# Sixteen of 24 attention chunks: q and k transposed by DMA instead of on TensorE

## The chip, the cores and the metric

One core of a Trainium2 chip. The metric is device time in microseconds (us); the kernels are compared in alternating rounds on one chip. A ratio is the mean time of one kernel's fast runs over that of the other's of the same rounds, so it is not quite the ratio of the medians quoted beside it. All profiled runs told of here are in the fast state. In the profile lines PE is TensorE, PEld its weight loads, DVE VectorE, ACT ScalarE, POOL GpSimd and SP SyncE, which here issues DMAs; PSUM is the memory that this kernel's matmuls and transposes on TensorE write to.

## The reference, cut to what matters

Chunked linear attention with decay feeds a two-layer MLP with a piecewise activation:

```python
# B, H, S, D = 4, 8, 768, 64; reference works in blocks of 64, the kernel in chunks of 128 rows
intra = (q_b @ k_b.T * decay_mask) @ v_b          # per batch and head
inter = (q_b * lam_pow) @ kv_state
out   = intra + inter
kv_state = lam_block * kv_state + (k_b * rev_pow).T @ v_b
...
x = out.transpose(0, 2, 1, 3).reshape(3072, 512)
h = x @ w_in                                      # 512 -> 2048
g = where(h >= 1, h, where(h <= -1, 0, (h + 1)**2 / 4))
y = g @ w_out                                     # 2048 -> 512
```

## The kernel before

It has 24 chunks of 128 rows, and 6 MLP stages of 512 rows that take four chunks each. A list scheduler written in Python orders every engine's work before the program is built: each operation has an engine, an estimated duration in ns (plus `extra` until its result is there), the operations that it needs, and a due time. Engines then run their lists in that order. The estimates set the order and nothing else; a wrong one shows later as an engine standing at an instruction that isn't ready, with ready ones behind it (in the changed kernel ScalarE stood for 3.59 us at a v cast, while an eviction behind it had its matmuls done for 2.4 us of that).

```python
def cast(c, x, eng):          # GpSimd from chunk 4 on: q or k times its decay table, f32 -> bf16
    ...
def cast_v(c):                # ScalarE: v to bf16
    nc.scalar.copy(out=v_out(vi[c % NV]), in_=qkv_ld[c, 2].rearrange("p (a b) d -> p a b d", b=2))
def f_t(c):                   # PE: 8 transposes of 128x128 into PSUM
    for i, x in ((1, ks), (0, qs)):
        for hp in range(HP):
            nc.tensor.transpose(out=ptt[c][:, i, hp, :], in_=pair(x[c], hp), identity=ident)
def f_kb(c, hi):              # VectorE: transposed k into a zero-padded tile, twice a chunk
    nc.vector.tensor_copy(kbd[c % NKB][HD[hi], :, hi, :], ptt[c][HD[hi], 1])
def f_qT(c, e):               # VectorE (ScalarE for the first chunks): transposed q to SBUF
    ...
# the plan: loads book 1.19 us of the DMA queue and land 1.4 us after; 6 buffers each for q, k, v
add(("ld", i, x), "DMA", 1190, ..., [("cast", i - LD, x), ...], extra=1400, due=pos_)
add(("cast", c, 2), "ACT", 640, lambda c=c: cast_v(c), [("ld", c, 2), ("o", c - NV), ("u", c - NV), ("cast", c - 1, 2)])
add(("r", n1), "ACT", 690, ...)   # ScalarE: evict one block of the first MLP layer from PSUM
```

All loads of q, k and v and all stores are issued from SP, in one in-order queue (in the changed kernel SP stood for 1.31 us at a transpose whose cast was not done, with the next load behind it); the weights come through GpSimd's queue. ScalarE also evicts every block of both MLP layers, so what stands in front of an eviction on ScalarE can stop PE: the program has two PSUM tiles for the first layer, and in the changed kernel PE waited 2.4 us in all for their evictions `r`.

Of the kernel before, what the change touches and what calls it, by code (L numbers as in the profile page):

```python
# [9 lines left out]
BF16 = mybir.dt.bfloat16  # L10
# [13 lines left out]
def kernel(  # L24
# [16 lines left out]
    nc = tc.nc  # L41
# [3 lines left out]
    HP = H // 2  # L45
# [8 lines left out]
    CPS = MS // C  # L54

    LD = 6
    RW, NR = 2, 3
    DBG = False

    const = ctx.enter_context(tc.tile_pool(name="const", bufs=1))  # L60
    big = ctx.enter_context(tc.tile_pool(name="big", bufs=1))
    ld = ctx.enter_context(tc.tile_pool(name="ld", bufs=LD))
    qkp = ctx.enter_context(tc.tile_pool(name="qkp", bufs=3))
    qtp = ctx.enter_context(tc.tile_pool(name="qtp", bufs=3))
    scp = ctx.enter_context(tc.tile_pool(name="scp", bufs=3))
    xp = ctx.enter_context(tc.tile_pool(name="xp", bufs=3))
    gp = ctx.enter_context(tc.tile_pool(name="gp", bufs=2))
# [31 lines left out]
        out=causal, in_=causal, compare_op=AX.is_ge, fill=0.0,  # L99
# [3 lines left out]
    NKB, NUB, NV = 3, 3, 4  # L103
    kbd = [const.tile([128, HP, 2, 128], BF16, name=f"kbd{i}") for i in range(NKB)]
# [47 lines left out]
    LAT, FILL = 70, 170  # L152
# [6 lines left out]
    def add(key, eng, ns, fn, needs=(), due=None, extra=0):  # L159
        OPS[key] = Op(key, eng, ns, fn, needs, due, extra)  # L160
        ops.append(OPS[key])

    def run_plan(free):
# [36 lines left out]
        for t, _, x in sorted(out_seq, key=lambda p: p[:2]):  # L200
            if DBG:
                print(f"{t / 1e3:9.3f} {x.due / 1e3:9.3f} {x.eng:5s} {x.ns:6.0f} {x.key}")
            x.fn()

    def mm(*cols):
        return sum(c / 2.4 + 3 for c in cols)


    qs, ks, qT, sc_sb, xT, ptt, pst, pot = {}, {}, {}, {}, {}, {}, {}, {}
    pu = [None]  # L210
    HD = [slice(0, 64), slice(64, 128)]

    def pair(t, hp):
        return t[:, 2 * hp:2 * hp + 2, :].rearrange("p a d -> p (a d)")

    def cast(c, x, eng):
        tab, d, nm = ((tab_q, qs, "qs"), (tab_k, ks, "ks"))[x]
        t = qkp.tile([128, H, D], BF16, name=nm, tag=nm)
        eng.tensor_tensor(t, qkv_ld[c, x], _bc(tab[:, c % NCB, :], 2, D), op=AX.mult)  # L219
        d[c] = t  # L220

    def cast_v(c):
        nc.scalar.copy(out=v_out(vi[c % NV]), in_=qkv_ld[c, 2].rearrange("p (a b) d -> p a b d", b=2))  # L223

    def f_t(c):
        ptt[c] = pp_t.tile([128, 2, HP, 128], BF16, name="pt", tag="pt")
        for i, x in ((1, ks), (0, qs)):
            for hp in range(HP):
                nc.tensor.transpose(out=ptt[c][:, i, hp, :], in_=pair(x[c], hp), identity=ident)  # L229

    def f_kb(c, hi):
        nc.vector.tensor_copy(kbd[c % NKB][HD[hi], :, hi, :], ptt[c][HD[hi], 1])  # L232

    def f_qT(c, e):
        qT[c] = qtp.tile([128, HP, 128], BF16, name="qT", tag="qT")
        (nc.scalar.copy if e == "ACT" else nc.vector.tensor_copy)(qT[c], ptt[c][:, 0])  # L236

    def f_u(c):
        if c % NCB == 0:
            pu[0] = pp_u.tile([128, HP, 128], F32, name="pu", tag="pu")  # L240
        for hp in range(HP):
            nc.tensor.matmul(pu[0][:, hp, :], lhsT=pair(ks[c], hp), rhs=v_pair(vi[c % NV], hp),  # L242
                             start=(c % NCB == 0 and hp == 0), stop=True, skip_group_check=True)

    def f_ub(c, hi):
        nc.scalar.copy(out=ubd[c % NUB][HD[hi], :, HD[hi]], in_=pu[0][HD[hi], :, HD[hi]])

    def f_s(c, g):
        pst[c, g] = pp_s.tile([128, 4, 128], F32, name="ps", tag="ps")
        for j in range(2):  # L250
            for hi in range(2):
                nc.tensor.matmul(pst[c, g][:, 2 * j + hi, :], lhsT=kbd[c % NKB][:, 2 * g + j, hi, :],  # L252
                                 rhs=qT[c][:, 2 * g + j, :], start=True, stop=True)

    def f_m(c, g):
        if g == 0:
            sc_sb[c] = scp.tile([128, 2 * HP, 128], BF16, name="sc", tag="sc")
        nc.vector.tensor_tensor(sc_sb[c][:, 4 * g:4 * g + 4, :], pst[c, g], _bc(causal, 1, 4), op=AX.mult)  # L258

    def f_o(c):  # L260
        cb = c % NCB
        po = pot[c] = pp_o.tile([128, HP, 128], F32, name="po", tag="po")
        for hp in range(HP):
            if cb > 0:
                nc.tensor.matmul(po[:, hp], lhsT=ubd[(c - 1) % NUB][:, hp, :], rhs=qT[c][:, hp, :],  # L265
                                 start=True, stop=False)
            for hi in range(2):
                nc.tensor.matmul(po[:, hp], lhsT=vi[c % NV][:, hp, hi].rearrange("p a d -> p (a d)"),  # L268
                                 rhs=sc_sb[c][:, 2 * hp + hi, :], start=(cb == 0 and hi == 0), stop=(hi == 1))

    def f_x(c):
        sx, off = c // CPS, (c % CPS) * C
        if sx not in xT:
            xT[sx] = xp.tile([128, KO, MS], BF16, name="xT", tag="xT")
        nc.scalar.copy(out=xT[sx][:, :, off:off + C], in_=pot[c])  # L275
# [77 lines left out]
    def o_due(c):  # L353
        s, i = c // CPS, c % CPS
        if s == 0:
            return T0 - LEAD - (CPS - 1 - i) * 3550
        if s in QS:
            return l_due[1, s, 0, i] - LEAD
        return first[s] - LEAD - (CPS - 1 - i) * (first[s] - first[s - 1]) / CPS
# [12 lines left out]
    for kind, i in order:  # L372
        if kind == "w":
            for j in range(WS):
                add(("wi", i, j), "POOL", 900, lambda i=i, j=j: (load_w_in, load_w_out)[i](j),
                    [("cast", CPS - 2 + min(j, 1), 0), ("cast", CPS - 2 + min(j, 1), 1), ("wi", i, j - 1)] if i == 0 else [("cast", CPS, 1), ("cast", CPS, 0) if j else None, ("wi", i, j - 1)],
                    due=j + 4 * i)
# [9 lines left out]
    for c in range(NCH):  # L387
        od, cb = o_due(c), c % NCB
        lastu = c - 1 if cb else c - 2
        for x in (1, 0):  # L390
            e = "DVE" if c < CPS and x == (0 if c == CPS - 1 else 1) else "POOL"
            add(("cast", c, x), e, 690 if e == "DVE" else 1060,
                lambda c=c, x=x, eng=(nc.vector if e == "DVE" else nc.gpsimd): cast(c, x, eng),
                [("ld", c, x), ("t", c - 3), ("u", c - 3), ("cast", c - 1, x)])
        add(("cast", c, 2), "ACT", 640, lambda c=c: cast_v(c),
            [("ld", c, 2), ("o", c - NV), ("u", c - NV), ("cast", c - 1, 2)])
        add(("t", c), "PE", mm(*[128] * 8), lambda c=c: f_t(c),
            [("cast", c, 0), ("cast", c, 1), ("kb", c - 1, 0), ("kb", c - 1, 1), ("qT", c - 1)], due=od - 6000, extra=FILL)
        for hi in range(2):
            add(("kb", c, hi), "DVE", 365, lambda c=c, hi=hi: f_kb(c, hi), [("t", c), ("s", c - NKB, 1)])  # L400
        e = "ACT" if c < CPS else "DVE"
        add(("qT", c), e, 600 if c < CPS else 365, lambda c=c, e=e: f_qT(c, e), [("t", c), ("o", c - 3), ("qT", c - 1)])
        if cb < NCB - 1:
            add(("u", c), "PE", mm(*[128] * 4), lambda c=c: f_u(c),
                [("cast", c, 1), ("cast", c, 2), ("ub", lastu, 0), ("ub", lastu, 1), ("u", lastu)], due=od - 4000, extra=FILL)
            for hi in range(2):
                add(("ub", c, hi), "ACT", 372, lambda c=c, hi=hi: f_ub(c, hi), [("u", c), ("o", c - NUB + 1)])
        for h in range(2):
            add(("s", c, h), "PE", mm(*[128] * 4), lambda c=c, h=h: f_s(c, h),
                [("kb", c, 0), ("kb", c, 1), ("qT", c), ("m", c, 0) if h else ("m", c - 1, 1)],  # L410
                due=od - 3000 + 1000 * h, extra=FILL)
            add(("m", c, h), "DVE", 690, lambda c=c, h=h: f_m(c, h), [("s", c, h), ("o", c - 3), ("m", c, 0) if h else None])
        add(("o", c), "PE", mm(*[128] * (12 if cb else 8)), lambda c=c: f_o(c),
            [("m", c, 1), ("cast", c, 2), ("ub", c - 1, 0) if cb else None, ("ub", c - 1, 1) if cb else None,
             ("x", c - 1), ("o", c - 1)], due=od, extra=FILL)
        add(("x", c), "ACT", 600, lambda c=c: f_x(c), [("o", c), ("x", c - 1), ("l1", (c // CPS - 2) * FO - 1)])
# [65 lines left out]
```

## Time and profile before

| | before |
|---|---|
| time, median of 4 runs | 238.21 us |
| span of the profiled run | 234.8 us |
| PE slots in the program (worked out as in the prediction, 0.0563 us for 128 columns, 0.2163 us for 512) | 208.8 us |
| span less slots: PE waiting, start and end included | 26.0 us |
| ScalarE waiting for v loads, 60 to 165 us | 2.7 us |

"Span less slots" is the figure to follow through this document. The change takes 7.2 us of slots away; whatever else happens to the time is a change in PE's waiting. The profiled run of this kernel was the shortest of its four (236.26 us), so differences from its 26.0 us can be up to about 2 us too large. The page's own lines are in the prediction. One view that the prediction did not show is ScalarE's waits between 60 and 165 us (who waited for whom: us in total, times, longest):

```profile
ACT vi_127 L223 <- DMA x2f<-in_v_dram: 1.1, 2, 0.7
ACT vi_129 L223 <- DMA x2f<-in_v_dram: 1.0, 1, 1.0
ACT vi_126 L223 <- DMA x2f<-in_v_dram: 0.6, 1, 0.6
```

`x2f` is the loaded v and `vi` its cast: before the change ScalarE hardly ever reaches a v cast ahead of its load.

### The profile page before, as it was taken

To read this page: it belongs to the slowest core of one execution; us is meant where nothing else is said; L and a number is where in the kernel's file an instruction comes from. 1 tells how busy PE (TensorE), PEld (TensorE's weight loads), DVE (VectorE), ACT (ScalarE), POOL (GpSimd) and SP (SyncE) were. 2 spreads that over 40 slices of the span, in tenths; PEclk is the share of its full clock that TensorE was granted. 3 is DMA by queue.
4 is the path that set the end of the run, shared out by engine and by line. 5 is a ranking of instruction groups with operands and counts; after the bars stand their busy time and mean duration, and the time that the engine had idled before them with its cause. 6 is when DMAs were issued, how large, how long until landed. Compare 5 with 4: busy or idle time off the path is not lost.

```text
span 234.8 us, 4665 instructions
## 1 busy us (share of the span) xinstructions
PE 213.8 (91%) x1876; PEld 137.1 (58%) x1904; DVE 160.3 (68%) x274; ACT 123.4 (53%) x216; POOL 59.4 (25%) x64
## 2 busy tenths in 40 slices
PE   0487997999997999999999999999999999999993
PEld 0476633575896997777765455555555454444441
DVE  7587399957499999885776876876766835545300
ACT  3456566243577766666566366566455354544110
POOL 6562071061366548303303403302000000000000
PEclk9999999999999999999999999999999999999999
DMA  6999969986999999899993011011011011110212
GB/s 139 220 212 200 192 112 185 196 162 186 247 201 218 227 221 206 191 243 228 230 255 81 19 45 37 12 45 47 0 45 47 0 45 47 45 43 2 92 51 83
DMA packets 82725, 29.67 MB, mean 126 GB/s; under 512 B 75536, under 2 KB 79632, under 8 KB 82704
## 3 DMA queue, kind: packets, MB, share of 16 engines
q1 hardware_dynamic: 78336, 25.17, 48.2%
q0 software_dynamic: 4224, 4.19, 11.1%
q8 instruction: 15, 0.25, 0.4%
q14 instruction: 6, 0.05, 0.1%
q10 hardware_dynamic: 144, 0.00, 0.0%
HBM read 27.27 MB, written 6.29 MB: 143 GB/s over the span
## 4 chain that ended last, share of the span: by engine, by line
PE 75%; DVE 16%; ACT 3%; DMA 2%; issue 2%; SPq 0%; ACTq 0%
PE py L323 33%; PE ph L295 26%; PE ps L252 5%; DVE gT L315 4%; PE pt L229 4%; PE po L268 4%; DMA x2f<-in_v_dram 2%; DVE sc L258 2%; PE pu L242 2%; PE po L265 2%; ACT r L303 1%; DVE kbd_121 L232 1%; PE ph L288 1%; DVE kbd_120 L232 1%; DVE qT L236 1%
## 5 line engine op out<-in xcount | busy, mean ns | idle before, releaser
L303 ACT ACTIVATE r<-ph,one 128x512 bf16<-128x512 f32 x94 | 64.1, 687 | 57.6 <-PE ph L295 40.9
L295 PE MATMUL ph<-xT,w_in_sb 128*128 128x128 bf16 (+1 forms) x744 | 93.1, 269 | 1.0 <-ACT r L303 0.4
L323 PE MATMUL py<-w_out_sb,gT 128*128 128x512 bf16 x364 | 91.5, 379 | 0.9
L295 PEld LDWEIGHTS <-w_in_sb 128*128 128x128 bf16 x752 | 53.0, 98 | 28.0 <-issue 1.4
L323 PEld LDWEIGHTS <-gT 128*128 128x128 bf16 x384 | 35.4, 98 | 33.3 <-DVE gT L315 0.2
L219 POOL TENSOR_TENSOR ks<-x1f,tab_k 128x512 bf16<-128x512 f32 x21 | 24.0, 1141 | 93.0 <-DMA x1f<-in_k_dram 38.9
L258 DVE TENSOR_TENSOR sc<-ps,causal 128x512 bf16<-128x512 f32 x48 | 33.0, 687 | 19.0 <-PE ps L252 18.8
L219 POOL TENSOR_TENSOR qs<-x0f,tab_q 128x512 bf16<-128x512 f32 x23 | 25.8, 1123 | 7.0 <-DMA x0f<-in_q_dram 6.9
L328 ACT COPY osb<-py 128x512 f32<-128x512 f32 x24 | 14.1, 586 | 20.6 <-PE py L323 20.0
L275 ACT CAST xT<-po 128x512 bf16<-128x512 f32 x24 | 14.0, 585 | 11.9 <-PE po L268 11.8
L242 PEld LDWEIGHTS <-ks 128*128 128x128 bf16 x80 | 6.2, 105 | 9.7 <-DVE ks L219 7.1
L229 PE MATMUL pt<-ident,ks 128*128 128x128 bf16 x96 | 10.1, 232 | 0.1
L229 PE MATMUL pt<-ident,qs 128*128 128x128 bf16 x96 | 10.0, 231 | 0.0
L229 PEld LDWEIGHTS <-ks 128*128 128x128 bf16 x96 | 7.7, 106 | 3.3 <-issue 0.3
L252 PE MATMUL ps<-qT,kbd_121 128*128 128x128 bf16 x64 | 6.8, 229 | 3.0 <-DVE qT L236 1.7
L242 PE MATMUL pu<-vi_126,ks 128*128 128x128 bf16 x24 | 2.5, 232 | 7.7 <-ACT vi_126 L223 7.7
L236 DVE COPY qT<-pt 128x512 bf16<-128x512 bf16 x20 | 8.5, 425 | 0.3
L252 PEld LDWEIGHTS <-kbd_121 128*128 128x128 bf16 x64 | 4.9, 102 | 5.8 <-DVE kbd_121 L232 2.6
L252 PE MATMUL ps<-qT,kbd_120 128*128 128x128 bf16 x64 | 6.8, 229 | 1.4 <-ACT qT L236 1.1
L232 DVE COPY kbd_120<-pt 64x512 bf16<-64x512 bf16 x16 | 6.7, 418 | 1.7 <-PE pt L229 0.9
L252 PE MATMUL ps<-qT,kbd_122 128*128 128x128 bf16 x64 | 6.5, 225 | 1.3 <-DVE qT L236 0.8
L252 PEld LDWEIGHTS <-kbd_120 128*128 128x128 bf16 x64 | 4.8, 102 | 3.8 <-DVE kbd_120 L232 1.8
(207 smaller groups left out, 246.4 us busy)
## 6 DMA issues: line engine op xcount, KB each, us to landing
x1f<-in_k_dram SPq DMA_DIRECT2D x24, 256.0 KB, 4.6
x0f<-in_q_dram SPq DMA_DIRECT2D x24, 256.0 KB, 4.8
x2f<-in_v_dram SPq DMA_DIRECT2D x24, 256.0 KB, 4.7
out_dram<-osb SPq DMA_DIRECT2D x24, 256.0 KB, 2.0
w_in_sb<-in_moe_w_in_dram POOLq DMA_DIRECT2D x4, 512.0 KB, 8.3
w_out_sb<-in_moe_w_out_dram POOLq DMA_DIRECT2D x4, 512.0 KB, 8.3
lam_b<-in_lam_dram ACTq DMA_DIRECT2D x1, 4.0 KB, 3.3
```

The source lines that it names most:

```text
L219: eng.tensor_tensor(t, qkv_ld[c, x], _bc(tab[:, c % NCB, :], 2, D), op=AX.mult)
L229: nc.tensor.transpose(out=ptt[c][:, i, hp, :], in_=pair(x[c], hp), identity=ident)
L232: nc.vector.tensor_copy(kbd[c % NKB][HD[hi], :, hi, :], ptt[c][HD[hi], 1])
L236: (nc.scalar.copy if e == "ACT" else nc.vector.tensor_copy)(qT[c], ptt[c][:, 0])
L242: nc.tensor.matmul(pu[0][:, hp, :], lhsT=pair(ks[c], hp), rhs=v_pair(vi[c % NV], hp), start=(c % NCB == 0 and hp == 0), stop=True, skip_gr ...
L252: nc.tensor.matmul(pst[c, g][:, 2 * j + hi, :], lhsT=kbd[c % NKB][:, 2 * g + j, hi, :], rhs=qT[c][:, 2 * g + j, :], start=True, stop=True)
L258: nc.vector.tensor_tensor(sc_sb[c][:, 4 * g:4 * g + 4, :], pst[c, g], _bc(causal, 1, 4), op=AX.mult)
L275: nc.scalar.copy(out=xT[sx][:, :, off:off + C], in_=pot[c])
L295: nc.tensor.matmul(ph[:, j * m:(j + 1) * m], lhsT=w_in_sb[:, ko, (ni + j) * 128:(ni + j + 1) * 128], rhs=xT[s][:, ko, part * m:(part + 1) ...
L303: nc.scalar.activation(out=r_t[grp][:, i, :], in_=ph_t[s, ni, part], func=AF.Relu, bias=one[:, 0:1])
L323: nc.tensor.matmul(py_t[s, ms], lhsT=gT[s][:, ko, ms * 128:(ms + 1) * 128], rhs=w_out_sb[:, ko, :], start=(ko == 0), stop=(ko == FO - 1))
L328: nc.scalar.copy(out=osb[s, ms], in_=py_t[s, ms])
```

## The change

The intent: PE is full (91% busy), the transposes and their PSUM copies take PE and VectorE time (0.0563 us a transpose, 0.42 us a copy), and a DMA can transpose between SBUF tiles (the page after the change lists 32 `DMA_TRANSPOSE`). From chunk 8 on, both transposes become DMAs on SP, and the padding copies read SBUF.

```diff
+    XT, NQT = 2 * 4, 3
...
     def f_kb(c, hi):
-        nc.vector.tensor_copy(kbd[c % NKB][HD[hi], :, hi, :], ptt[c][HD[hi], 1])
+        nc.vector.tensor_copy(kbd[c % NKB][HD[hi], :, hi, :], ptt[c][HD[hi], 1] if c < XT else kT[c][HD[hi]])
...
+    def f_kx(c):
+        kT[c] = qtp.tile([128, HP, 128], BF16, name="kT", tag="kT")
+        nc.sync.dma_start_transpose(out=kT[c], in_=ks[c].rearrange("p h d -> p (h d)"))
+    def f_qx(c):
+        qT[c] = qtp.tile([128, HP, 128], BF16, name="qT", tag="qT")
+        nc.sync.dma_start_transpose(out=qT[c], in_=qs[c].rearrange("p h d -> p (h d)"))
...
+        if c < XT:
             add(("t", c), "PE", mm(*[128] * 8), lambda c=c: f_t(c), ...)
...
+        else:
+            add(("t", c), "DMA", 620, lambda c=c: f_kx(c), [("cast", c, 1), ("kb", c - NQT, 0), ("kb", c - NQT, 1)], due=-2, extra=1600)
+            add(("qT", c), "DMA", 620, lambda c=c: f_qx(c), [("cast", c, 0), ("o", c - NQT)], due=-2, extra=1600)
         for hi in range(2):
-            add(("kb", c, hi), "DVE", 365, ...)
+            add(("kb", c, hi), "DVE", 365 if c < XT else 285, ...)
```

More of the change, by code (lines that the diff above doesn't have):

```diff
@@ L63 @@
     qkp = ctx.enter_context(tc.tile_pool(name="qkp", bufs=3))
-    qtp = ctx.enter_context(tc.tile_pool(name="qtp", bufs=3))
+    qtp = ctx.enter_context(tc.tile_pool(name="qtp", bufs=NQT))
     scp = ctx.enter_context(tc.tile_pool(name="scp", bufs=3))
@@ L206, in mm @@
         return sum(c / 2.4 + 3 for c in cols)
-    qs, ks, qT, sc_sb, xT, ptt, pst, pot = {}, {}, {}, {}, {}, {}, {}, {}
+    qs, ks, kT, qT, sc_sb, xT, ptt, pst, pot = {}, {}, {}, {}, {}, {}, {}, {}, {}
     pu = [None]
@@ L393 @@
                 lambda c=c, x=x, eng=(nc.vector if e == "DVE" else nc.gpsimd): cast(c, x, eng),
-                [("ld", c, x), ("t", c - 3), ("u", c - 3), ("cast", c - 1, x)])
+                [("ld", c, x), ("cast", c - 1, x), ("t", c - 3), ("u", c - 3) if x else ("qT", c - 3)])
         add(("cast", c, 2), "ACT", 640, lambda c=c: cast_v(c),
             [("ld", c, 2), ("o", c - NV), ("u", c - NV), ("cast", c - 1, 2)])
-        add(("t", c), "PE", mm(*[128] * 8), lambda c=c: f_t(c),
-            [("cast", c, 0), ("cast", c, 1), ("kb", c - 1, 0), ("kb", c - 1, 1), ("qT", c - 1)], due=od - 6000, extra=FILL)
+        if c < XT:
+            add(("t", c), "PE", mm(*[128] * 8), lambda c=c: f_t(c),
+                [("cast", c, 0), ("cast", c, 1), ("kb", c - 1, 0), ("kb", c - 1, 1), ("qT", c - 1)], due=od - 6000, extra=FILL)
+            e = "ACT" if c < CPS else "DVE"
+            add(("qT", c), e, 600 if c < CPS else 365, lambda c=c, e=e: f_qT(c, e), [("t", c), ("o", c - NQT), ("qT", c - 1)])
+        else:
+            add(("t", c), "DMA", 620, lambda c=c: f_kx(c), [("cast", c, 1), ("kb", c - NQT, 0), ("kb", c - NQT, 1)], due=-2, extra=1600)
+            add(("qT", c), "DMA", 620, lambda c=c: f_qx(c), [("cast", c, 0), ("o", c - NQT)], due=-2, extra=1600)
         for hi in range(2):
-            add(("kb", c, hi), "DVE", 365, lambda c=c, hi=hi: f_kb(c, hi), [("t", c), ("s", c - NKB, 1)])
-        e = "ACT" if c < CPS else "DVE"
-        add(("qT", c), e, 600 if c < CPS else 365, lambda c=c, e=e: f_qT(c, e), [("t", c), ("o", c - 3), ("qT", c - 1)])
+            add(("kb", c, hi), "DVE", 365 if c < XT else 285, lambda c=c, hi=hi: f_kb(c, hi), [("t", c), ("s", c - NKB, 1)])
         if cb < NCB - 1:
```

## The prediction

> **What bounds the kernel now.** I read the page first, then the windows, then the PE timeline, then the SP and GpSimd timelines, since those two would carry the change.
>
> ```profile
> PE 213.8 (91%) x1876; PEld 137.1 (58%) x1904; DVE 160.3 (68%) x274; ACT 123.4 (53%) x216; POOL 59.4 (25%) x64
> ...
> PE   0487997999997999999999999999999999999993
> ...
> DMA  6999969986999999899993011011011011110212
> ...
> PE 75%; DVE 16%; ACT 3%; DMA 2%; issue 2%; SPq 0%; ACTq 0%
> ...
> L229 PE MATMUL pt<-ident,ks 128*128 128x128 bf16 x96 | 10.1, 232 | 0.1
> L229 PE MATMUL pt<-ident,qs 128*128 128x128 bf16 x96 | 10.0, 231 | 0.0
> ...
> L236 DVE COPY qT<-pt 128x512 bf16<-128x512 bf16 x20 | 8.5, 425 | 0.3
> ```
>
> The tensor engine is busy 91% of the span and from slice 8 on it is full; the DMA engines are as full up to slice 21 (about 122 us) and nearly idle after. The L229 rows seem to price the transposes at 20.1 us for 192, 105 ns each. That price is wrong for a saving, because a busy time counts each group's pipeline tail, which the next group overlaps. The PE timeline gives the slot that a transpose really takes:
>
> ```profile
> 73.48 0.40 PE L252 MATMUL ps<-qT,kbd_122 128*128 128x128 bf16 x4 [0.56 <-DVE qT L236]
> 73.72 0.39 PE L229 MATMUL pt<-ident,ks 128*128 128x128 bf16 x4
> 73.94 0.39 PE L229 MATMUL pt<-ident,qs 128*128 128x128 bf16 x4
> ...
> 227.78 2.97 PE L323 MATMUL py<-w_out_sb,gT 128*128 128x512 bf16 x13
> ```
>
> Four transposes move the next group on by 0.22 us, so one slot is 0.056 us, though the group shows 0.39. For 512 columns, (2.97-0.38)/12 = 0.216 us. Is PE really full? The score products of chunk 8 start at 73.48, the last of chunk 23 at 186.52 (this group is the last of its line in the trace): 113.0 us. In program order 787 matmuls of 128 columns and 316 of 512 lie between: 787 x 0.0563 + 316 x 0.2163 = 112.7 us (the slots with one more digit). From 73 us on PE therefore waits for almost nothing; each slot removed there is time removed, each new wait there is time added. The 16% of DVE in the chain of waits is links between already full stretches; I give nothing for it.
>
> [...]
>
> **The change part by part.** Removed: on PE, 16 chunks x 8 transposes x 0.0563 us = 7.2 us of slots, all behind 73 us except chunk 8's and 9's, which stand just before. On DVE, 16 q copies x 0.425 = 6.8 us; the 32 padded-k copies read SBUF instead of PSUM and may drop from the 0.42 us that the L232 rows show. DVE is not what PE waits for in this stretch, so neither is counted. Moved: transposes leave PE's in-order queue, so PE has no place where it must wait for a cast for their sake.
>
> Added: 32 DMA transposes of 128 KB on the SP queue. Estimate of one: the plan in the kernel books 0.62 us of the DMA engines, half of a load of 256 KB (loads land 1.2 us apart in the full stretch), and 1.6 us to landing. I take that, plus an estimated 0.7 us of issue on SP, between the 0.36 us of a store and the about 1.1 us of a queued load. Bytes in all: 32 x 0.62 = 20 us of DMA. The loads would then end near 142 us and not 122; the last chunk's scores are due at about 177 (184.5 less the 7.2), so bandwidth alone does not bind.
>
> What matters is order. SP issues in order, and in the changed program it is: k load of the next chunk, q transpose of this one, q load, v load of the next, k transpose of the next. A transpose waits for the GpSimd cast, the cast for the load, and the loads behind wait for the transpose. Loads that ran three or four in flight now run at most one chunk ahead, so each chunk costs a full round trip:
>
> ```profile
> 43.87 0.37 SPq L364 DMA_DIRECT2D x1f<-in_k_dram  x1
> ...
> 47.61 1.04 POOL L219 TENSOR_TENSOR ks<-x1f,tab_k 128x512 bf16<-128x512 f32 x1 [11.46 <-DMA x1f<-in_k_dram]
> ...
> 64.27 1.04 POOL L219 TENSOR_TENSOR ks<-x1f,tab_k 128x512 bf16<-128x512 f32 x1 [2.35 <-DMA x1f<-in_k_dram]
> 65.46 1.04 POOL L219 TENSOR_TENSOR qs<-x0f,tab_q 128x512 bf16<-128x512 f32 x1 [0.15 <-PE ph L295]
> 67.85 1.29 POOL L219 TENSOR_TENSOR ks<-x1f,tab_k 128x512 bf16<-128x512 f32 x1 [1.35 <-DMA x1f<-in_k_dram]
> ```
>
> The first two rows are a load in a nearly empty queue: 3.7 us from issue to the start of its cast. The next are the casts of chunk 8 (k, q) and 9 (k), one chunk each 3.6 us. The new round: 3.7 load + 1.2 cast + 0.2 handover + 0.7 issue of the transpose = 5.8 us per chunk (the DMA work of a round, 3 x 1.2 + 2 x 0.62 = 4.8, fits in it).
>
> Against that, the need. Summing PE's slots in the changed order and setting them on the same clock (start = slots before it + 21.4 us, which fits chunk 8 and 16 of the trace within 0.4), the scores of chunks 8 to 15 are due at 73.9, 79.1, 82.2, 86.9, 90.6, 96.2, 102.9, 111.3 us, then each 8.3 us. The supply: q of chunk 8 is cast at 66.5; its transpose is issued at 66.6, finds some queue, and lands near 69.5. Two rounds are stretched or squeezed by the queue, so I put chunk 9 at 74.6 and chunk 10 at 80.3, then a round of 5.8 each: chunk 11 at 86.1, 12 at 91.9, 13 at 97.7, 14 at 103.5, 15 at 109.3. The latest against need is chunk 13, 1.5 us, plus 0.3 for the padding copy and semaphores: PE stands still for 1.8 us once (a stall shifts all that follows, so it is the largest lag and not the sum). From chunk 15 on supply runs ahead again.
>
> Sum: 238.2 - 7.2 + 1.8 = 232.8 us, 2.3% faster.
>
> **The rivals.** First, the transposes cost what is booked or less and the round is 5.2 us: no lag, 238.2 - 7.2 = 231.0, down to 229.5 if a few waits in the stretch from 60 to 73 us go too. For it: [...] PE had 3 to 4 us in hand at chunk 8. Against: nothing in hand at chunk 11 and 12.
>
> Second, the SP queue takes PE's place as the bound between chunks 9 and 15. If one transpose holds SP, or the DMA engines, for 2 us and not 0.7, the round is about 7.2 us; chunk 14 would land at 80.3 + 4 x 7.2 = 109.1 (chunks 9 and 10 later too, by 2 to 3 us) against 102.9: 8 to 9 us of stall, the gain is eaten and the time is 239 to 241. For it: the change has a long chain through four queues, and DMA is above 90% busy in slices 7 to 20. Against: the next stage needs a chunk only each 8.3 us, so a round of up to 8 us stops hurting after chunk 15.
>
> Third, a transpose is much slower than a copy [...], over 4 us: the round passes 8.3 us, PE starves through chunk 23, and each us of round beyond that costs 10 us or more: 250 and up. [...]
>
> Fourth, the reading of the busy column: 128 x 105 ns = 13.4 us, 225 us. The timeline speaks against it: slots, not busy time, are what is freed.
>
> **Range and chances.** The middle case is 232.8, hardly past the 2% line (233.5), so faster and same are nearly even; the unknown cost of a transpose has its tail on the slow side only, and the gain is capped at about 8 us. Range 229.5 to 247. Faster 0.47, within 2% 0.31, slower 0.22.
>
> **What would show it.** The pt groups of PE fall from 192 to 64 instructions and q copies on DVE from 20 to 4. The issue list shows the transposes' time to landing: 2 to 3 us is my case, over 4 the third rival. The distance from one k cast on GpSimd to the next for chunks 9 to 14 should be near 5.8 us; 5 or less means the first rival, 7 and more the second. Waits of PE for kbd or qT behind DMA transposes should total under 3 us; SP's own waits should name GpSimd casts. In the windows, the DMA share stays high to about 140 us. I am wrong if PE saves 13 us, if DVE turns out to set the time, or if the transposes' own cost and not their place in the queue decides.

## The result, and the profile after

244.94 us (median of 4 runs, 244.22 to 245.97) against 238.21: ratio 1.0296, 95% interval 1.022 to 1.0372. Slower by 3%, where 2.3% faster was foretold; 244.94 is inside the range given, the direction is wrong. The span of the profiled run is 243.2 us and the program's slots are 201.6, so PE's waiting grew from 26.0 to 41.6 us: 15.6 us more (13.9 by the medians, 244.94 - 238.21 + 7.2), where 1.8 was expected. From the page of the changed kernel:

```profile
PE 210.6 (87%) x1776; PEld 129.0 (53%) x1776; DVE 155.2 (64%) x258; ACT 121.3 (50%) x216; POOL 61.5 (25%) x64
...
PE   0477997999989796899969897799999999999992
...
PEclk9999999999999999999999999799999999999999
DMA  6999979948989887989979889933210111100211
...
q1 hardware_dynamic: 95744, 29.37, 57.9%
...
PE 45%; DMA 21%; DVE 10%; SPq 9%; POOL 5%; issue 4%; ACT 4%; POOLq 0%; ACTq 0%
...
L233 DVE COPY kbd_122<-kT 64x512 bf16<-64x512 bf16 x12 | 3.4, 286 | 5.1 <-DMA kT<-ks 5.0
...
kT<-ks SPq DMA_TRANSPOSE x16, 3.0
qT<-qs SPq DMA_TRANSPOSE x16, 3.0
```

PE's row has holes from slice 12 to 26, where only slice 13 had one before. The chain of waits passed through PE for 75% before; now 45%, with DMA, SP and GpSimd taking 35%. The padding copy became cheaper as hoped (286 to 337 ns, by tile, against 418). A transpose lands 3.0 us after its issue: the page's row for it is unremarkable, and the trouble is not there.

The SP queue (start, duration, what was issued) shows the round that the prediction described:

```profile
72.75 0.43 SPq L373 DMA_DIRECT2D x1f<-in_k_dram  x1
74.01 1.19 SPq L245 DMA_TRANSPOSE qT<-qs  x1
75.25 0.57 SPq L373 DMA_DIRECT2D x0f<-in_q_dram  x1
75.87 0.58 SPq L373 DMA_DIRECT2D x2f<-in_v_dram  x1
77.76 1.19 SPq L241 DMA_TRANSPOSE kT<-ks  x1
79.00 0.58 SPq L373 DMA_DIRECT2D x1f<-in_k_dram  x1
```

k load, q transpose, q load, v load, k transpose, next k load. SP stands still between 76.45 and 77.76, because the k transpose waits for a cast of a load issued at 72.75. A transpose holds SP for 1.19 us. The casts of k on GpSimd for chunks 9 to 12 give the length of a round:

```profile
69.24 1.32 POOL L220 TENSOR_TENSOR ks<-x1f,tab_k 128x512 bf16<-128x512 f32 x1 [2.37 <-PE py L332]
76.66 1.08 POOL L220 TENSOR_TENSOR ks<-x1f,tab_k 128x512 bf16<-128x512 f32 x1 [2.67 <-DMA x1f<-in_k_dram]
82.47 1.04 POOL L220 TENSOR_TENSOR ks<-x1f,tab_k 128x512 bf16<-128x512 f32 x1 [1.85 <-DMA x1f<-in_k_dram]
89.44 1.57 POOL L220 TENSOR_TENSOR ks<-x1f,tab_k 128x512 bf16<-128x512 f32 x1 [2.78 <-PE ph L304]
```

From chunk 9 (69.24) to chunk 16 (115.36 in the same view) it is 46.1 us, 6.6 us per chunk; the prediction said 5.8. Before, the same seven rounds took 28.7 us, 4.1 each. But 6.6 us is still faster than the 8.3 us at which PE uses chunks from 15 on, and yet PE lost more there. The scores of chunk 15 start 28.2 us later than the slots before them, those of chunk 19 start 37.2 us later: 9.0 us lost (about 1.7 of them to a half clock, told of at the end) in a stretch where transposed q and k lay ready (those of chunk 19 landed by 143.6, their scores start at 159.7). ScalarE's and VectorE's waits, 60 to 165 us, tell why:

```profile
ACT vi_127 L224 <- DMA x2f<-in_v_dram: 8.7, 4, 3.6
ACT vi_126 L224 <- DMA x2f<-in_v_dram: 8.1, 3, 3.6
ACT vi_129 L224 <- DMA x2f<-in_v_dram: 8.0, 4, 3.0
...
ACT vi_128 L224 <- DMA x2f<-in_v_dram: 4.6, 4, 1.9
...
DVE kbd_122 L233 <- DMA kT<-ks: 5.0, 3, 3.3
DVE kbd_120 L233 <- DMA kT<-ks: 4.3, 4, 2.5
DVE kbd_121 L233 <- DMA kT<-ks: 2.0, 2, 1.1
```

ScalarE now waits 29.4 us for v loads (2.7 before), VectorE 11.3 us for transposed k. What PE itself waits for between 115 and 165 us is not q or k but work that stands behind these waits, VectorE's masks and ScalarE's evictions (`xT`, 0.9 us, is the third and last row):

```profile
PE po L277 <- DVE sc L267: 3.5, 3, 1.3
PE ph L304 <- ACT r L312: 2.0, 3, 0.8
```

One such moment, in the timeline (the bracket is the idle time before it and what ended it):

```profile
145.09 0.62 ACT L224 CAST vi_126<-x2f 128x512 bf16<-128x512 f32 x1 [3.59 <-DMA x2f<-in_v_dram]
...
145.71 0.59 DVE L233 COPY kbd_122<-kT 64x512 bf16<-64x512 bf16 x2 [3.32 <-DMA kT<-ks]
...
146.09 0.69 ACT L312 ACTIVATE r<-ph,one 128x512 bf16<-128x512 f32 x1
...
146.84 0.59 PE L304 MATMUL ph<-xT,w_in_sb 128*128 128x512 bf16 x2 [0.68 <-ACT r L312]
```

The v cast is that of chunk 20 and stands on ScalarE 3.6 us before its load lands, though the scores of chunk 20 start only at 168.0. The evictions `r` that PE needs stand behind it. The plan put the cast there because by its estimates the load would have been in.

### The profile page after: what moved, and what is told of

It is laid out like the page before. It is cut to its first block, busy times and chain, and to the rows that moved or that the text cites. A ratio compares the mean times of both kernels' runs of the same rounds, so it can differ in the third digit from the quotient of the medians.

```text
span 243.2 us, 4467 instructions
## 1 busy us (share of the span) xinstructions
PE 210.6 (87%) x1776; PEld 129.0 (53%) x1776; DVE 155.2 (64%) x258; ACT 121.3 (50%) x216; POOL 61.5 (25%) x64
## 3 DMA queue, kind: packets, MB, share of 16 engines
q1 hardware_dynamic: 95744, 29.37, 57.9%
## 4 chain that ended last, share of the span: by engine, by line
PE 45%; DMA 21%; DVE 10%; SPq 9%; POOL 5%; issue 4%; ACT 4%; POOLq 0%; ACTq 0%
PE py L332 23%; PE ph L304 15%; DMA x0f<-in_q_dram 10%; DMA x2f<-in_v_dram 8%; SPq L245 4%; DMA x1f<-in_k_dram 4%; POOL qs L220 3%; SPq L241 3%; DVE gT L324 2%; PE ps L261 2%; POOL ks L220 2%; PE po L277 2%; DVE sc L267 2%; SPq L373 1%; ACT r L312 1%
## 5 line engine op out<-in xcount | busy, mean ns | idle before, releaser
L304 PE MATMUL ph<-xT,w_in_sb 128*128 128x128 bf16 (+1 forms) x752 | 94.2, 271 | 3.7 <-ACT r L312 2.4
L332 PE MATMUL py<-w_out_sb,gT 128*128 128x512 bf16 x384 | 95.5, 382 | 0.0
L312 ACT ACTIVATE r<-ph,one 128x512 bf16<-128x512 f32 x94 | 64.0, 688 | 46.1 <-PE ph L304 30.1
L304 PEld LDWEIGHTS <-w_in_sb 128*128 128x128 bf16 x752 | 53.6, 98 | 34.6 <-issue 7.0
L220 POOL TENSOR_TENSOR ks<-x1f,tab_k 128x512 bf16<-128x512 f32 x21 | 25.0, 1191 | 73.0 <-DMA x1f<-in_k_dram 55.7
L220 POOL TENSOR_TENSOR qs<-x0f,tab_q 128x512 bf16<-128x512 f32 x23 | 26.6, 1158 | 33.2 <-DMA x0f<-in_q_dram 20.3
L251 PEld LDWEIGHTS <-ks 128*128 128x128 bf16 x80 | 6.1, 102 | 11.4 <-DVE ks L220 7.5
L261 PE MATMUL ps<-qT,kbd_121 128*128 128x128 bf16 x64 | 6.5, 219 | 5.2 <-DVE kbd_121 L233 2.6
L261 PE MATMUL ps<-qT,kbd_120 128*128 128x128 bf16 x64 | 6.8, 229 | 3.4 <-DVE sc L267 1.4
L261 PEld LDWEIGHTS <-kbd_121 128*128 128x128 bf16 x64 | 4.6, 97 | 8.6 <-DVE kbd_121 L233 3.4
L224 ACT CAST vi_126<-x2f 128x512 bf16<-128x512 f32 x6 | 3.7, 616 | 10.3 <-DMA x2f<-in_v_dram 10.3
L224 ACT CAST vi_127<-x2f 128x512 bf16<-128x512 f32 x6 | 3.7, 619 | 9.2 <-DMA x2f<-in_v_dram 9.2
L261 PEld LDWEIGHTS <-kbd_120 128*128 128x128 bf16 x64 | 4.8, 101 | 6.0 <-issue 2.0
L224 ACT CAST vi_129<-x2f 128x512 bf16<-128x512 f32 x6 | 3.7, 620 | 8.0 <-DMA x2f<-in_v_dram 8.0
L261 PE MATMUL ps<-qT,kbd_122 128*128 128x128 bf16 x64 | 6.3, 219 | 1.1 <-DVE sc L267 1.1
L233 DVE COPY kbd_122<-kT 64x512 bf16<-64x512 bf16 x12 | 3.4, 286 | 5.1 <-DMA kT<-ks 5.0
L261 PEld LDWEIGHTS <-kbd_122 128*128 128x128 bf16 x64 | 4.7, 98 | 3.4 <-issue 1.4
```

The costliest lines, as they stand in the source:

```text
L220: eng.tensor_tensor(t, qkv_ld[c, x], _bc(tab[:, c % NCB, :], 2, D), op=AX.mult)
L251: nc.tensor.matmul(pu[0][:, hp, :], lhsT=pair(ks[c], hp), rhs=v_pair(vi[c % NV], hp), start=(c % NCB == 0 and hp == 0), stop=True, skip_gr ...
L261: nc.tensor.matmul(pst[c, g][:, 2 * j + hi, :], lhsT=kbd[c % NKB][:, 2 * g + j, hi, :], rhs=qT[c][:, 2 * g + j, :], start=True, stop=True)
L304: nc.tensor.matmul(ph[:, j * m:(j + 1) * m], lhsT=w_in_sb[:, ko, (ni + j) * 128:(ni + j + 1) * 128], rhs=xT[s][:, ko, part * m:(part + 1) ...
L312: nc.scalar.activation(out=r_t[grp][:, i, :], in_=ph_t[s, ni, part], func=AF.Relu, bias=one[:, 0:1])
L332: nc.tensor.matmul(py_t[s, ms], lhsT=gT[s][:, ko, ms * 128:(ms + 1) * 128], rhs=w_out_sb[:, ko, :], start=(ko == 0), stop=(ko == FO - 1))
```

## The experiments

Two theories at the start. A: the transposes' *place* in the in-order SP queue (they wait for casts, and the loads wait behind them). B: the transposes' own *cost*, 1.19 us of SP each and, by the page, (57.9% of 243.2 - 48.2% of 234.8) / 32 = 0.86 us of all DMA engines each (an estimate from the time that packets took; it takes loads and stores to cost what they did before). Later two forms of A: A1, PE lacks the scores' operands; A2, the in-order lists of ScalarE and VectorE stand at things not needed yet.

**Transposes left out.** Every engine's order kept, the scores read the untransposed tiles (wrong result on purpose).

```diff
-        kT[c] = qtp.tile(...); nc.sync.dma_start_transpose(out=kT[c], in_=ks[c]...)
+        kT[c] = ks[c].rearrange("p (a b) d -> p a (b d)", b=2)          # the same for qT
-    qkp = ... bufs=3
+    qkp = ... bufs=6
```

> The changed kernel with every engine's order kept, but the 32 transposes simply left out: scores read the untransposed tiles (wrong result on purpose). No wait and no DMA cost. Both theories (A: the transposes' place in the in-order SP queue; B: the transposes' own cost on SP and the DMA engines) expect the pure gain of the freed PE slots, 238.2 - 7.2 = 231.0 us (230 to 232). Above 234 the order of PE itself is to blame, and both fall.

Measured 232.92 us, ratio 0.9748 (0.9688 to 0.9809). By the ratio 6.0 us are saved, close to the price of 7.2 us and far from the 13.4 us of the busy column. Span less slots is 29.9, 3.9 more than in the profiled run before (1.2 by the ratio), so the new order seems to cost something by itself, mostly at chunk 10, where PE waits for VectorE's masks; the other 11.7 of the 15.6 us come with the transposes. The scores follow the slots by 25.6 us at chunk 15 and by 25.8 at chunk 23, so most of the loss that comes with the transposes lies behind chunk 15 (28.2 there in the changed kernel, 37.2 at chunk 19). Its round is 5.75 us: the pace at which this program draws chunks when no transpose stands in SP's queue.

**Cost without wait.** The transposes read a constant tile (wrong result on purpose).

```diff
+    still = const.tile([128, H * D], BF16); nc.gpsimd.memset(still, 0.0)
-        nc.sync.dma_start_transpose(out=kT[c], in_=ks[c].rearrange("p h d -> p (h d)"))
+        nc.sync.dma_start_transpose(out=kT[c], in_=still)               # the same for qT
```

> Same order of all engines, all 32 transposes are issued, but from a tile that never changes (wrong result on purpose), so that SP does not wait for GpSimd's casts; cost without wait. A: loads run ahead again, ACT's waits for the v loads fall from 29 us (60 to 165 us) to under 6, and the time is 231 to 234 us. B: 1.2 us of SP and 0.9 us of DMA for each are still paid, 241 to 245 us.

Measured 235.12 us, ratio 0.9841 (0.9777 to 0.9905). B's number is missed by 6 us or more. A's is missed a little: 31.4 us less slots, and ScalarE still waits 12.7 us for v. The run is not free of waits: SP's transposes no longer wait for GpSimd, but between 60 and 165 us they wait 28.1 us for VectorE and PE, whose work frees the three buffers each of transposed k and q. Against B it counts all the same, as the cost is paid in full (the median issue took 1.56 us here).

**Wait without cost.** Ordinary SBUF-to-SBUF copies in the same places (wrong result on purpose).

```diff
-        nc.sync.dma_start_transpose(out=kT[c], in_=ks[c].rearrange("p h d -> p (h d)"))
+        nc.sync.dma_start(out=kT[c].rearrange("p a d -> p (a d)"), in_=ks[c].rearrange("p h d -> p (h d)"))
```

> Same order and the same waits for the casts, but each transpose is an ordinary SBUF-to-SBUF copy of the same tile (wrong result on purpose); wait without most of the cost. A: the round per chunk falls only by the shorter issue, from 6.6 to about 5.8 us, so most of the loss stays: 236 to 241 us, ACT still waits over 15 us for v loads. B: 231 to 233 us.

Measured 234.86 us, ratio 0.9849 (0.9772 to 0.9926). A is missed: with every wait in place (SP waits 33.8 us for casts, 25.5 in the changed kernel), nearly all the loss is gone. So neither theory stands alone. A copy holds SP for 0.47 us and the round is 5.93 us; without the waits for casts it is 5.98; the changed kernel has both and 6.6. Taking out either one is enough, and both rounds come near the 5.75 us of the left-out kernel. This suggests a pace between 6.0 and 6.6 us per chunk up to which the program bears the supply. An estimate of where: on ScalarE 20 evictions stand between the v casts of chunk 16 and chunk 23, 2.9 per chunk; a chunk's worth of MLP is 4 evictions and 8.3 us of PE, so these lists expect a chunk each 2.9/4 x 8.3 = 5.9 us. At 6.6 us they fall 0.7 us behind per chunk, about 10 us over 15 chunks, and the two single-cost kernels do lie 10.2 and 11.1 us of waiting below the changed one. That fits, but no run varied the pace alone, and 6.6 was measured for chunks 9 to 16, 2.9 counted for 16 to 23.

**Other place, same cost.** The transposes of a chunk go behind the loads of the chunk two further on. Correct result.

```diff
+            late = OPS["ld", min(c + 2, NCH - 1), 2].own + 0.5
-            add(("t", c), "DMA", 620, ..., due=-2, extra=1600)          # and qT
+            add(("t", c), "DMA", 620, ..., due=late, extra=1600)
```

> Correct result. The plan places the transposes of a chunk behind the loads of the chunk two further on, so SP seldom waits for a cast; same cost, other place. A: 231 to 235 us, waits of SP for GpSimd under 8 us (26 us now). B: 240 us or more.

Measured 236.75 us, ratio 0.9959 (0.9921 to 0.9998), a miss of both: better than the change by 8 us, hardly a gain over before. SP's waits for GpSimd fell to 17.0 us, not under 8. The round is 5.74 us, but ScalarE still waits 10.4 us for v, and VectorE 8.0 us for transposed k, which now comes later.

**Late v casts.** A2 can be tried without touching the supply: only the plan's order of ScalarE changes. Correct result.

```diff
-            [("ld", c, 2), ("o", c - NV), ("u", c - NV), ("cast", c - 1, 2)])
+            [("ld", c, 2), ("o", c - NV), ("u", c - NV), ("cast", c - 1, 2), ("s", c - 1, 0) if c >= XT else None])
```

> Correct result. All as in the change, but in the plan the v cast of a chunk on ScalarE stands behind the scores of the chunk before it, near its use, and no longer where the plan thought the load would be in; loads and transposes keep their rules. Theory A2 (late loads hurt because ScalarE and VectorE stand in order behind a v load or a transposed k that they do not need yet): ScalarE's waits for v loads fall from 29 us to under 10, and the time from 245 to 237 to 240 us (what VectorE's waits cost stays). Theory A1 (PE lacks the scores' operands themselves): no change, 243 to 246 us.

Measured 244.67 us, ratio 1.0243 (1.0171 to 1.0316): no change. Taken alone that is what A1 expects. The waits say otherwise: ScalarE's fell from 29.4 to 13.4 us, VectorE's for transposed k rose from 11.3 to 15.1. The trace shows the second queue holding PE: VectorE stands 4.1 us at a padding copy, a mask stands behind it, and PE waits 4.2 us for the mask.

```profile
132.99 0.28 DVE L233 COPY kbd<-kT 64x512 bf16<-64x512 bf16 x1 [4.08 <-DMA kT<-ks]
136.50 0.37 PE L277 MATMUL po<-sc,vi 128*128 128x128 bf16 x2 [4.17 <-DVE sc L267]
```

The first queue was freed in part, and the second, with the same fault, held PE.

**Late v casts and late padding copies.** Correct result.

```diff
+            # as above, and:
-            add(("kb", c, hi), "DVE", ..., [("t", c), ("s", c - NKB, 1)])
+            add(("kb", c, hi), "DVE", ..., [("t", c), ("s", c - NKB, 1), ("s", c - 1, 1) if c >= XT else None])
```

> Correct result. As the one before, and the padding copies of k on VectorE also stand behind the scores of the chunk before. A2: waits for v loads and transposed k both under 6 us together after 110 us, and 233 to 236 us. A1: 243 to 246 us.

Measured 238.11 us, ratio 1.0011 (0.9985 to 1.0037): 6.8 us recovered, short of the 233 to 236 expected. The supply is as slow as in the changed kernel, 6.76 us per chunk, and loads and transposes keep their order in SP's queue, so this gain comes from the order of the engines that use them. (The plan, made anew, also moved 52 of PE's 296 operations; the control below speaks against a gain from that.) GpSimd's k casts of chunks 9 to 12:

```profile
69.01 1.04 POOL L220 TENSOR_TENSOR ks<-x1f,tab_k 128x512 bf16<-128x512 f32 x1 [1.89 <-DMA x1f<-in_k_dram]
76.96 1.22 POOL L220 TENSOR_TENSOR ks<-x1f,tab_k 128x512 bf16<-128x512 f32 x1 [3.41 <-DMA x1f<-in_k_dram]
83.28 1.04 POOL L220 TENSOR_TENSOR ks<-x1f,tab_k 128x512 bf16<-128x512 f32 x1 [3.31 <-DMA x1f<-in_k_dram]
90.08 1.04 POOL L220 TENSOR_TENSOR ks<-x1f,tab_k 128x512 bf16<-128x512 f32 x1 [3.58 <-PE ph L304]
```

and what is left of ScalarE's waits for v, 60 to 165 us (VectorE's for transposed k are gone):

```profile
ACT vi L224 <- DMA x2f<-in_v_dram: 8.8, 5, 3.8
```

From chunk 13 on, scores follow the slots with 29.1 to 30.3 us, without the climb to 37.2. The rest is one stall of 3 us near chunk 12, where the v load itself was late (the 3.8 us above), and a clock drop behind it (told of at the end).

**The plan's numbers.** Only the estimates change. Correct result.

```diff
-            add(("ld", i, x), "DMA", 1190, ..., extra=1400, due=pos_)
+            add(("ld", i, x), "DMA", 1190, ..., extra=2400, due=pos_)
-            add(("t", c), "DMA", 620, ...)                              # and qT
+            add(("t", c), "DMA", 900, ...)
```

> Correct result. Only the plan's numbers for DMAs differ: a load lands 2.4 us behind its slot (1.4 before), a transpose takes 0.9 us of the queue (0.62 before). The plan then orders all engines for a slower supply. If the loss is the plan's optimism meeting in-order engines, 232 to 236 us; if it is the cost of the transposes as such (27 us of DMA, 38 us of SP), 240 us or more.

Measured 238.35 us, ratio 0.9992 (0.9966 to 1.0017). Three constants recover 6.6 us although the round stays at 6.81 us: the supply is no faster. What in the order did it is not shown, as the new numbers also re-sort SP's queue and 128 of PE's 296 operations. ScalarE's waits for v are 7.3 us, VectorE's for transposed k 4.3. It falls between the two expectations: 33.3 us less slots, some of it at the start, where the new numbers delay chunk 4 by 3 us.

**Fewer chunks.** Chunks 16 to 23 only. Correct result.

```diff
-    XT, NQT = 2 * 4, 3
+    XT, NQT = 4 * 4, 3
```

> Correct result. Only chunks 16 to 23 are transposed by DMA, when the loads have run ahead: saves 8 x 8 x 0.0563 = 3.6 us of PE, 234.6 us if nothing is lost; A2 expects some loss from loads that slow down at the end, 234 to 237 us; a loss by the transposes' cost alone would be half of the change's, 238 to 242 us.

Measured 237.29 us, ratio 0.9949 (0.9914 to 0.9985), just above what A2 expected. With slots of 205.2 us, 29.6 are waiting.

**Combinations.** Late order with the plan's numbers, late order with the transposes behind the loads of the next chunk (0.9 us booked for each), and late order with chunks 16 to 23 only. All correct; the edits are those above, with `c + 1` in place of `c + 2` in the second.

> Correct result. Both repairs: v casts and padding copies stand near their use, and the plan reckons with slower DMAs (2.4 us to landing of a load, 0.9 us for a transpose). If the two act on the same loss, no better than one of them, 236 to 238 us; if the plan's numbers also mend the order of loads, 233 to 235 us and faster than before.

> Correct result. Late v casts and padding copies, and the transposes stand behind the loads of the next chunk (plan: 0.9 us each). The stall that the late order left at chunk 12 and 13 came from a v load behind the transposes; here it goes first: 233 to 236 us.

> Correct result. Only chunks 16 to 23 by DMA, with late v casts and padding copies for these: 3.6 us of PE saved, waits of ScalarE and VectorE for DMA near zero after 110 us: 234 to 236 us.

Measured 237.16 us, ratio 0.9967 (0.9942 to 0.9993); 235.20 us, ratio 0.9891 (0.9862 to 0.9921); 234.84 us, ratio 0.9891 (0.9852 to 0.9931). The first adds little (1 us): both repairs treat the same loss. The second and third beat the kernel before by 1.1% and the changed one by about 4%, and are the best correct versions here. In the second ScalarE waits 0.6 us for v between 60 and 165 us and VectorE not at all for transposed k, although its round, 6.45 us, is nearly that of the changed kernel. (Its loads also stand ahead of the transposes, so it does not show which of the two edits did it.) It still waits 31.5 us in span less slots, 5.5 more than the profiled run before (4.6 by the ratio), which is most of the 7.2 us that it saves.

**Control.** The kernel before with the late order.

```diff
+            # both edits of the late order, `if c >= 8`, in the kernel before
```

> Control, correct result. The kernel before, with the same late order of v casts and padding copies for chunks 8 to 23 and all transposes on PE. Its loads are early, so theory A2 expects nothing: 237 to 239.5 us, the same. If it is faster by 2% or more, the late order is a gain of its own and what it did to the changed kernel does not show where the loss came from.

Measured 239.54 us, ratio 1.006 (1.0029 to 1.0092). Slightly slower, so the late order is no gain of its own; what it gave the changed kernel is loss repaired.

| kernel | time, us | span less slots | us per chunk, 9 to 16 | ScalarE for v, 60 to 165 | VectorE for transposed k |
|---|---|---|---|---|---|
| before | 238.21 | 26.0 | 4.1 | 2.7 | - |
| changed | 244.94 | 41.6 | 6.6 | 29.4 | 11.3 |
| left out | 232.92 | 29.9 | 5.75 | 1.5 | - |
| cost, no wait for casts | 235.12 | 31.4 | 5.98 | 12.7 | 3.5 |
| wait, no cost | 234.86 | 30.5 | 5.93 | 11.6 | 2.5 |
| late v casts | 244.67 | 39.7 | 6.63 | 13.4 | 15.1 |
| late v casts and copies | 238.11 | 34.8 | 6.76 | 8.8 | 0 |

## Why the prediction was wrong

- *The price of a transpose, 0.0563 us, 7.2 us in all*: right. The program's slots fell from 208.8 to 201.6, and with the transposes left out the time fell by 2.5% (6.0 us), the most seen in any run.
- *PE waits for almost nothing from 73 us on, so each new wait is time added*: right ("from slice 8 on it is full" overlooks slice 13, but that lies before 76 us), and it is what made the loss so large.
- *The round trip through one SP queue*: the mechanism is right, the size is not. The step that failed first is "3.7 load + 1.2 cast + 0.2 handover + 0.7 issue of the transpose = 5.8 us". It was 6.6: the rounds of chunks 10 to 16 are 3.9 load + 1.2 cast + 0.2 between the steps + 1.2 issue = 6.5 us from load to load. The issue of a transpose, estimated at 0.7, makes 0.5 of the difference. Alone this would not have turned the sign: with 6.6 us the prediction's own sums put chunk 13 at 100.1 us against 96.2, a stall of 4.2 us and 235.2 us in all.
- *"From chunk 15 on supply runs ahead again"*, and in the second rival "a round of up to 8 us stops hurting after chunk 15": this is the step that turned the sign. It compared supply with the moment at which PE needs the scores' operands. The program needs a chunk when the in-order lists of ScalarE and VectorE reach its v cast and its padding copies, and the plan had put those near the time at which it believed the loads to be in, a chunk each 5.9 us. Against the left-out kernel the scores lost 2.6 us up to chunk 15, not far from the 1.8 foretold, and 9 more by chunk 19. The late order, with a supply no faster, brought 6.8 us back.
- *"DVE is not what PE waits for in this stretch, so neither is counted"*: true before, false after; VectorE waited 11.3 us for transposed k, and with late v casts alone its waits were 15.1 us and the whole loss stayed.
- *0.62 us of the DMA engines per transpose*: 0.86. That alone (32 x 0.86 = 28 us) would have moved the end of the loads from 122 to 150 us; with SP's waits it came near 160, not 142. Bandwidth did not bind by itself, as expected: with no less cost and no waits for casts the time was 235.1.
- *The second rival* named SP as the bound with a round of 7.2 us, and 239 to 241 us. It was the nearest of the four, with the wrong end to the loss.

What stays open: why the left-out kernel has 3.9 us more waiting than before was only read from its trace, not tried. The padding copies were not moved alone, and neither more buffers for the transposed tiles nor another engine's queue for the transposes was tried.

## What to carry to other kernels

The busy column priced a matmul of 128 columns at twice its slot here (105 against 56 ns); take the price from the start of one group to the start of the next. When work moves to an in-order DMA queue whose entries wait for compute, every load behind them moves too (here the round went from 4.1 to 6.6 us per chunk); then look not only at the last consumer but at where each in-order engine *stands in line* for those loads, and place such instructions by need and not by expected arrival. Freeing only one of two engines with that fault can show nothing at all (244.67 us here, against 244.94).

## What else the runs measured

- A transpose of 128 KB from SBUF to SBUF took 0.86 us of the 16 DMA engines (152 GB/s), beside loads, and 1.23 by the same sum in the run with a constant tile ((65.5% of 232.9 - 113.2) / 32); copies of the same tile in the same places took (54.2% of 232.1 - 113.2) / 32 = 0.39 us. All three are estimates of that kind.
- Such a transpose held SP for 1.19 us here, against 0.47 for the copy, and took 3.0 us from issue to landing (median); the one issued at 168.44 us in the changed kernel, in an idle queue, took 2.4.
- At 128 columns this kernel sustains 56 ns a matmul, with a weight load for each (four and four in 0.22 us, at 73.72 us before the change).
- Three traces show the granted clock at half for a while. In the late-order kernel PE was idle for 2.9 us, then had half clock for 3.4 us from 102.6 us; with late v casts alone it was idle for 4.2 us, then had half clock for 3.4 us. The changed kernel dropped to half clock for 3.4 us at 154.1 us with no gap above 1.3 us, after 4 us in which PE was busy for 2.14, so a gap as long as those of the other two is not needed for it. No run varied the gaps, and what sets the drop off is not shown:

```profile
150.00:154.00 4.00, 2.14 (x13) 0.94 (x11) 2.21 (x4) 3.39 (x7) 1.09 (x2) 1.00 1.06 196
154.00:158.00 4.00, 3.74 (x13) 1.60 (x13) 2.96 (x6) 1.20 (x2) 0.92 (x1) 0.57 1.31 216
```

The columns are the stretch, its length, the busy time of PE, its weight loads, VectorE, ScalarE and GpSimd, the granted clock (0.57), the DMA share and GB/s. Half a clock for 3.4 us is worth about 1.7 us of the 15.6.
